# A fused memory-attention and MLP block: v's weights and the first q, k slices loaded ahead of the second 256 rows, scale steps in PSUM, finer unread products, the last tile in halves, a new order

## The chip, the cores and the metric

The kernel runs on one core of one Trainium2 chip. The metric is the device time of one execution in microseconds (us). A profile is one execution recorded by the hardware profiler. Engines: PE is TensorE (PEld its weight loads), DVE is VectorE, ACT is ScalarE, POOL is GpSimd, and SP issues DMAs. L12 is line 12 of the kernel's file; the changed file has other line numbers from L310 on (mostly one more, from L866 on five to six more).

## The reference

`x` has 2048 rows (tokens) of 512 columns. The result is the sum of three terms, all on the same rows:

```python
xn = layernorm(x)
return x + A(xn, wq, wk, wv, wo, beta) + B(xn, w1, b1, w2, b2)
# A: 32 heads of 16, 4 segments of 512 rows, run in order
for s in range(4):
    logits = qs @ ks.T / 4 + mask             # mask: -1e9 for keys behind the query
    a_dot  = softmax(logits) @ vs
    a_mem  = phi(qs) @ M / (phi(qs) @ z + 1e-6)
    o      = g * a_mem + (1 - g) * a_dot      # g = sigmoid(beta), one per head
    M, z   = M + phi(ks).T @ vs, z + phi(ks).sum(rows)
A = concat(o) @ wo                            # phi(t) = t + 1 if t > 0 else exp(t)
# B: a second layernorm, then
B = gelu(layernorm(xn) @ w1 + b1) @ w2 + b2   # 512 -> 1792 -> 512
```

## The kernel before, in words

**Number format.** Products with weights are done on f16 pairs. Each f32 matrix is split into a high part and the remainder (low part), and a product is three f16 products per block of 128 rows: high-high, high-low, low-high (`split3`, L583). So a projection of one 128-row slice of weights against 512 columns is 12 products, and so is a token tile of 128 rows against 512 columns of v's weights.

**Weights.** Before a weight can be split it has to be loaded (`w_load`, on SP's queue), its size has to be estimated from squares (`w_square`: ACT at L351, or products of blocks with themselves on PE at L380 whose diagonal DVE sums at L382; these are called traces below), and a power of two has to be made from that (`w_scale`, `qk_scale`: a small product with ones on PE, then the exponent steps at L386 and L390 on DVE). `w_split` then makes the two parts: in kind "V" ACT writes the high part (L445) and DVE the remainder (L446), in kind "G" POOL scales (L448), ACT copies (L450) and POOL subtracts (L452). The weights come in pieces: `qk` is the first 128 columns of wk and wq, `QK` the other three, `v` is wv, `1a`, `1b`, `2a`, `2b` the halves of w1 and w2, `o` is wo.

**Rows.** x comes in blocks of 256 rows (two tiles of 128). `norm_sums` and `norm_root` make mean and root, `norm_apply` normalizes, and `ln_out` transposes on PE (L561) and splits the result (L564 on ACT, L565 on DVE) into `xnT`. The first 512 rows are loaded in two blocks, the second of which is kept in the tiles nN and nD. In the kernel before the second block is normalized on POOL (L534), the first one on DVE (L532).

**Attention.** There are 16 units: 4 segments x 4 groups of 8 heads. A unit has its projections of q and k (job T, the low part Tv at L621), a round trip through DRAM that lays the heads out (`qk_rows`), the row maxima of the scores (jobs M: PE at L741, DVE at L748), their transposition (R, at L754), the scores (S at L783, exponents on ACT at L790, masks on POOL at L804), the products with v (`pv`, L817) and the normalization. For the first unit the projection of the first 256 rows stands alone (`first`, jobs Tp), ahead of that of the second 256 rows. V jobs make v for 128 tokens (12 products). The MLP runs between: jobs D (w1, evicted by DVE at L880), gelu, its split, and e (w2, L926, DVE at L930). At the end `out` multiplies by wo for a token tile (L944), DVE adds it to the tile (L947), and `save` stores it (L861).

**Order.** Nothing is scheduled automatically. Every stream of jobs (`streams`) has a letter, and the string `ORDER` says which stream is next; a job issues its instructions on the engines' queues, and each engine runs its queue in that order. A second string, `BANKS`, says which of PSUM's 8 banks each new tile (`dense`) gets; a job that gets a bank waits until the last reader of that bank is done. `hold` is a memset that makes the DMAs which reuse that memory wait for DVE. `warm` issues products of the identity with itself whose result nobody reads.

Of the kernel before, what the change touches and what calls it, by code (L numbers as in the profile page):

```python
# [9 lines left out]
F32 = mybir.dt.float32  # L10
# [22 lines left out]
NW = 8  # L33
# [25 lines left out]
def streams():  # L59
# [78 lines left out]
    "oamakrkkhbckkkk0h0bihehceddhff220ff22qhjkk2n1h1662gkkrp6237s7lg3k783w8th88999!x9u#k!w7#9$4$vRRv9R$9!3#R!#%k4J5"  # L138
    "WxkR%&RRzzz%(S%%Lz&WTzXU%Vst)L(uzz3%Tk)U&LvVYY(zTvU)z)VTz&L)Y(UYi3-YzVY*YYYk*K+-,X4zzyz**J5Y+YYYz-,6AAY-*5RAAA"
    "aBRB-RzzCBC.K.+C*C/,*A.+kAzRRR,zAA:WkRzAWz/.sRt.uzSy:TjRBwUBxBR.C.CCVCvDAbATEBFGAURwAvVARBRHxJYz/zCBCCTUICKzXA"  # L140
    "zYYzA:/VcYTURAzzsXBAz:VtiAYBvBSYYRzTzCCUuCCdDYvYz;YeEYVJT;FUVRfyRYfRY;;aATAzYbRUAzGAVYTBRcYAHzzdUBVBYeIYRSzz<z"
    "YYCCCKCz=AzYYYff>TUYYYAaAzjBsAAVtz<bYROBR<wTuyCNBCxCCA=AvDUY>RBREJPsVTYYFUGVTAuAvAHYtiwYzBzCxCBCICAzYNYRUAzAVB"
    "RYAzAvRzzzcvBCOSCBTUCCzzRYYLRDVYYEzFYzz<GzyYLYLHezATUIAMZAAAVQLBzBBWzCTCXKCCUzVAzdMJAzzsAAAMRBzMByBtCCuTCKCADA"
    "EPOwBFxAAvAvRNYZfYZfYBGUQRJBRYWCiVHKCICCzAYYzAAYBRAAzBSOYPXYYBzzzTsYzUztCuCaCCzzVYTwjxRUVTDRYYvbRzERUvVJFTURcY"
    "yWdYORYRYYSYNzeAAVYRiYTYBXYAzzYYRZUYAzAGYVRBTzzCKHBCIUCCAABVTzRWRAAXzRAUzzffRYBjVYYYTSzUQYysPBaVCCCtCADAEYBYwu"
    "AFTAGAYYxNYYBYBYQYCHCvObCICAAARvPJURABzBABszzzCCtCCLVuLTzcUVDvzzwxETdLeFzzzLGfRYYzfRHNUyVRTUVYRAAAYBRvYAAzIYMY"
    "ZBzzCBCCSKiCRAWzzaMYTYUAVzARJYbzcABABMQBYzzTUzZCCVCCTUKXsuMzYJRtDRPEyWwFxYAAAYYVGHTRQYUAABOvNIVYBRPBCCKXvCCAZA"
    "zYBYYzAAYBRAzzSjBesTzzzCCtduCUVCTDYURYYREwYzzvzxVYRTFGYJYUVYfYzRNZTyUVYYvRHRYYAAABYRYOfzAWzYSYYTYRUzAzBYYRQzzC"
    "IBCCCVzzAszAtTzURRYVAATAROWPvBUzRwRNBYyVYSXROBYCCTUXCVxCDTjAAYYYEYAFAABYGRYRYBRBHKvCIUCCCAzVATYzYYizzAsBzUzAVR"
    "QzARRTzBzBzCtCSCCPUDwLYExFYVvzGLyTYLNvLHIAAAMYzUAVzTYUYMzBzAYVMZQzZzzBCTCUOBCCAAstzzzYYYPwBWYzYAAABYVxYZNyvYBM"  # L150
    "CTCUCCvAABAYRRRDAEAzVBRFBGHRRQPWRCTCCICAjzAYUYsztAAWYXYVYzzAwvxzzBSzBXCBCTCUCDYVYTUYVYTvURYEzzVRTRYYNRRZzRRYYS"
    "FOYzUVzyATYYRUzAAGBVYYYYTHABXAzRBYUzzCCIVCCzzTAYRYUWVzAARYAzTARYBUVzBRRCSCBTUCCQDEXyVYYAAYTYFYGABPYABAYYBYHYCC"
    "UICCYAVAABYATYYBYAQUYYBCVCTUCCDEVYFYYGHYYIYYYYYYMMMZMZZZ"
# [4 lines left out]
    "01234567012345614526371052671034261705342617035426107356420735264071526540715402675430125673012657320614527036"  # L158
    "41752036475126347512034715623471625437164325741362534612054612704631720476231547361204367120436712430624751062"
    "41705241705617205436172436017236017620347620341576203145762031457632145176320475163204751632407513624057136240"  # L160
    "57162401572431507243107624531762541736257431602576403157640315640371564072561473265104765104736510427651024702"
    "63517305264137052641702614702351470623154706234710536427153642751036427513642735167340516735401564730215643725"
    "61437516437054317605431760543761054361205437205413725024513740256137425061742506314506310473152047361052170365"
    "27052431670524315627053614270361423761024671025671032567120536127410253645130243510624351067243167524316754236"
    "17542356417023564127035641270356120356142705164270514521670421657210465201476537206143720614206173540267302547"
    "03251403142650314261540356410235641027536142753641275036127503461250"
# [17 lines left out]
def infini_mixer_kernel(ctx: ExitStack, tc: tile.TileContext, x, wq, wk, wv, wo, beta, w1, b1, w2, b2, out):  # L184
# [71 lines left out]
    def col(j):  # L256
        return sc[:, j:j + 1]
# [148 lines left out]
    def w_scale(m):  # L406
# [8 lines left out]
        a = sm.tile([P, 2], F32, name="fa")  # L415
# [60 lines left out]
    def norm_root(h):  # L476
# [15 lines left out]
        nws[h] = ag, a  # L492
# [13 lines left out]
    def ratio(h):  # L506

        a = nws[h][1][:, 0]
# [351 lines left out]
    def save(tok):  # L860
        Q.dma_start(out[P * tok:P * tok + P, :], acc[tok])  # L861
# [186 lines left out]
```

## Time and profile before

| | us |
|---|---|
| median of 3 runs (lowest to highest) | 692.88 (692.62 to 693.17) |
| the profiled execution | 692.55 |
| its span, first to last instruction | 690.8 |
| PE busy | 680.1 |
| DVE busy | 504.6 |
| ACT busy | 472.2 |
| POOL busy | 353.1 |
| mean granted TensorE clock | 0.994 |

The span is 1.7 us shorter than the execution. Busy time of different engines overlaps. A matmul's duration in the profile includes its latency, so successive ones overlap as well: start to start, products of 512 columns follow at some 0.22 us, though one is recorded as 0.38. PEclk in the page is the granted clock in tenths, over 40 slices of 17 us.

### The profile page before, as it was taken

Reading aid. Unit: us, or ns where it says so; the run is one execution under the profiler, and the core shown is the slowest. Engines: PE = TensorE matmul, PEld = TensorE weight load, DVE = VectorE, ACT = ScalarE, POOL = GpSimd, SP = SyncE. Lnnn points to the kernel's source line nnn. Section 1 sums busy time; section 2 is a strip of 40 time slices with the busy share of each in tenths; the row PEclk is TensorE's granted clock in tenths of the full one; section 3 lists DMA queues with packets and bytes.
Section 4 is the critical chain, followed back from the end, with each engine's and each line's share of the span. In section 5 each row is a group of like instructions: output and inputs, shape, how many; then the busy total and the mean of one; then the engine's idle time right before and its main releaser. Section 6 shows DMA issues by size and latency. Waiting matters only on the chain.

```text
span 690.8 us, 15856 instructions
## 1 busy us (share of the span) xinstructions
PE 680.1 (98%) x5855; PEld 393.0 (57%) x5855; DVE 504.6 (73%) x1612; ACT 472.2 (68%) x877; POOL 353.1 (51%) x577
## 2 busy tenths in 40 slices
PE   6999999999999999999999999999999999999997
PEld 5854655657654566755546555565555447465543
DVE  5899978897787669867696786968577475688622
ACT  3688897987766577668836738667865555767970
POOL 7488649575535343564554345434462405438562
PEclk8999999999999999999999999999999999999999
DMA  9888233302321142322221224221402113420101
GB/s 269 264 207 205 97 94 58 99 30 76 76 47 40 34 116 58 107 48 79 69 70 26 77 57 101 70 64 44 105 18 56 55 48 94 102 77 17 18 2 61
DMA packets 52745, 55.84 MB, mean 81 GB/s; under 512 B 4974, under 2 KB 41596, under 8 KB 52668
## 3 DMA queue, kind: packets, MB, share of 16 engines
q1 hardware_dynamic: 50364, 50.64, 26.4%
q0 software_dynamic: 2304, 4.20, 3.8%
q8 instruction: 46, 0.75, 0.5%
q14 instruction: 31, 0.25, 0.1%
HBM read 37.77 MB, written 17.05 MB: 79 GB/s over the span
## 4 chain that ended last, share of the span: by engine, by line
PE 96%; POOL 1%; DVE 1%; issue 0%; POOLq 0%
PE dense L583 40%; PE dense L926 21%; PE dense L817 11%; PE dense L944 6%; PE dense L783 6%; PE dense L741 6%; PE dense L681 2%; PE dense L561 1%; PE dense L380 1%; PE dense L697 1%; PE dense L648 1%; DVE dense L748 1%; PE dense L718 1%; DVE w1s L446 0%; PE dense L754 0%; POOL kst L237 0%
## 5 line engine op out<-in xcount | busy, mean ns | idle before, releaser
L748 DVE CUSTOM_DVE_ANT_0 dense<-dense,mask 128x384 f32<-128x384 f32 (+3 forms) x512 | 233.8, 526 | 39.0 <-PE dense L741 34.4
L790 ACT ACTIVATE pt<-dense,qkcs 128x512 f32<-128x512 f32 (+1 forms) x384 | 204.0, 632 | 35.0 <-PE dense L783 35.0
L926 PE MATMUL dense<-w2s,hT 128*128 128x512 f16 x672 | 166.0, 380 | 0.0
L583 PE MATMUL dense<-xnT,w1s 128*128 128x256 f16 x1344 | 161.2, 273 | 0.0
L804 POOL TENSOR_SCALAR_AFFINE_SELECT pt<-pt 128x256 f32<-128x256 f32 x256 | 102.3, 436 | 108.8 <-ACT pt L790 108.3
L583 PEld LDWEIGHTS <-w1s 128*128 128x128 f16 x1344 | 129.5, 98 | 29.2 <-issue 5.4
L900 POOL TENSOR_TENSOR hT<-hh,hT 128x512 f16<-128x512 f32 x64 | 68.3, 1067 | 95.8 <-ACT hT L898 89.2
L926 PEld LDWEIGHTS <-hT 128*128 128x128 f16 x672 | 61.0, 98 | 67.3 <-issue 13.4
L817 PE MATMUL dense<-pt,vt 128*32 128x512 f32 (+3 forms) x1024 | 77.6, 436 | 0.0
L748 DVE DVE_READ_ACCUMULATOR2_ANT mc<- 128x1 f32 x512 | 72.6, 142 | 0.0
L880 DVE SCALAR_TENSOR_TENSOR hT<-dense,sc,cb 128x512 f32<-128x512 f32 x64 | 43.6, 681 | 34.2 <-PE dense L583 27.7
L898 ACT ACTIVATE hT<-hh 128x512 f16<-128x512 f32 x64 | 37.4, 584 | 27.1 <-POOL hh L896 27.1
L817 PEld LDWEIGHTS dense<-pt,vt 128*32 128x32 f32 x1024 | 30.7, 109 | 41.7 <-issue 31.8
L783 PE MATMUL dense<-qst,kst 50*128 50x384 f16 (+3 forms) x512 | 52.1, 298 | 1.1 <-DVE mc L748 1.1
L896 POOL TENSOR_SCALAR hh<-hT,sc 128x512 f32<-128x512 f32 x64 | 42.1, 658 | 21.2 <-ACT hT L886 17.9
L741 PE MATMUL dense<-kst,qst 48*128 48x384 f16 (+3 forms) x512 | 51.5, 298 | 0.0
L886 ACT ACTIVATE hT<-hT,b1t 128x256 f32<-128x256 f32 x112 | 46.4, 495 | 0.2
L848 POOL TENSOR_TENSOR nN<-nN,oT 128x512 f32<-128x512 f32 x16 | 21.0, 1312 | 49.5 <-DVE oT L660 49.5
L583 PE MATMUL dense<-xnT,wks 128*128 128x512 f16 (+1 forms) x252 | 44.5, 329 | 0.0
L583 PE MATMUL dense<-xnT,wqs 128*128 128x512 f16 (+1 forms) x252 | 44.4, 329 | 0.0
L944 PE MATMUL dense<-wos,oT 128*128 128x512 f16 x192 | 43.8, 379 | 0.0
L583 PE MATMUL dense<-wvs,xnT 128*128 128x512 f16 x192 | 43.8, 379 | 0.0
(230 smaller groups left out, 838.1 us busy)
## 6 DMA issues: line engine op xcount, KB each, us to landing
kst<-kd SPq DMA_DIRECT2D x32, 192.0 KB
qst<-qd SPq DMA_DIRECT2D x32, 192.0 KB
qd<-hl SPq DMA_DIRECT2D x36, 128.0 KB
kd<-hl SPq DMA_DIRECT2D x33, 128.0 KB
acc<-in_A_x_dram SPq DMA_DIRECT2D x16, 256.0 KB
acc<-in_B_b_dram POOLq DMA_DIRECT2D x16, 256.0 KB, 4.2
out_dram<-acc SPq DMA_DIRECT2D x16, 256.0 KB
xt<-in_A_x_dram SPq DMA_DIRECT2D x14, 256.0 KB
```

Source lines behind the costliest of these rows:

```text
L583: T.matmul(p, ws(k, a), xs(k, b), start=i == 0, stop=i == 3 * KT - 1)
L741: T.matmul(p[:, o:o + n], stk[i, 0][r, t, P * qb:P * qb + P], stk[i, 1][r, t, :n], start=True, stop=True)
L748: V.tensor_tensor_reduce(p[:, o:o + n], p[:, o:o + n], mask[:, 512 - n:], 1.0, -3e38, OP.add, OP.max, mc[i][:, 4 * b + t, qb:qb + 1])
L783: T.matmul(p[:, o:o + n], stk[i, 1][r, t, P * kb:P * kb + P], stk[i, 0][r, t, P * kb:], start=True, stop=True)
L790: A.activation(pt[i, 4 * b + t][:, OFF[kb]:OFF[kb] + n], p[:, c:c + n], AF.Exp, scale=qkcs[:, 1, i % NG:i % NG + 1])
L804: G.affine_select(v, v, pattern=[[0, 2], [1, P]], compare_op=OP.is_ge, fill=0.0, base=0, channel_multiplier=-1)
L817: T.matmul(p[32 * c:32 * c + 32, P * kb:], vt[s, kb][:, 4 * g + c, 16 * odd:16 * odd + 32], pt[i, 2 * c + odd][:, OFF[kb]:OFF[kb] + LEN[kb ...
L880: V.scalar_tensor_tensor(hzs[fh][:, f0:f + 1, :], p[:, :256 * n].rearrange("p (f c) -> p f c", f=n), col(CG + fh), cbt[hf].unsqueeze(1).to ...
L886: A.activation(hzs[j % 2][:, f, :], hzs[j % 2][:, f, :], AF.Gelu_apprx_tanh, bias=b1t[:, fo:fo + 1])
L900: G.tensor_tensor(hT[:, z, 1, :], hht[j, c], hT[:, z, 0, :], op=OP.subtract)
L926: T.matmul(p, t[:, u, P * a:P * a + P], w2s[:, fo, v, :], start=fi == 0 and n == 0, stop=fi == FH - 1 and n == 2)
L944: T.matmul(p, o[:, u, P * b:P * b + P], wos[:, g, v, :], start=i == 0, stop=i == 3 * NG - 1)
```

## The change

**Loads.** The loads were one stream; now each weight has its own (`load` + name), so that their order can be chosen freely. Before, SP's queue begins with all 512 rows, then the four slices of wk and wq, then wv:

```order
L546 DMA xt<-in_A_x_dram 128x512 x2
L546 DMA nN<-in_A_x_dram 128x512
L546 DMA nD<-in_A_x_dram 128x512
L290 DMA wks<-in_A_wk_dram 128x4x128
L290 DMA wqs<-in_A_wq_dram 128x4x128
L290 DMA wks<-in_A_wk_dram 128x4x128
L290 DMA wqs<-in_A_wq_dram 128x4x128
L290 DMA pt<-in_A_wk_dram 128x4x128
L290 DMA pt<-in_A_wq_dram 128x4x128
L290 DMA pt<-in_A_wk_dram 128x4x128
L290 DMA pt<-in_A_wq_dram 128x4x128
L318 DMA wvs<-in_A_wv_dram 128x2x512
```

The same place in the changed kernel (wvs and pt hold pieces of v's weights here, in wks, wqs and pt those of k and q; nN and nD are the second 256 rows):

```order
L547 DMA xt<-in_A_x_dram 128x512 x2
L318 DMA wvs<-in_A_wv_dram 128x2x512
L290 DMA wks<-in_A_wk_dram 128x4x128
L290 DMA wqs<-in_A_wq_dram 128x4x128
L310 DMA pt<-in_A_wv_dram 128x512 x2
L290 DMA wks<-in_A_wk_dram 128x4x128
L290 DMA wqs<-in_A_wq_dram 128x4x128
L290 DMA pt<-in_A_wk_dram 128x4x128
L290 DMA pt<-in_A_wq_dram 128x4x128
L547 DMA nN<-in_A_x_dram 128x512
L547 DMA nD<-in_A_x_dram 128x512
L290 DMA pt<-in_A_wk_dram 128x4x128
```

Half of v (512 KB) took the place of the second 256 rows, the rest of v follows the first slices, and the second rows come after three of the four slices of k and q.

**DVE in the start.** Before, from the memset of `hold` to the first weight splits; L472 and L473 are the means, L565 the splits of transposed rows, L382 the diagonal of wv's or wk's trace:

```order
L532 TENSOR_SCALAR xt<-xt,ag,stats 128x512 x2
L565 SCALAR_TENSOR_TENSOR xnT<-dense_224,xnT 128x4x128
L565 SCALAR_TENSOR_TENSOR xnT<-dense_231,xnT 128x4x128
L386 TENSOR_SCALAR fa<-dense_248 128x2
L390 TENSOR_SCALAR qksc<-fa 128x2 x4
L403 TENSOR_TENSOR qkcs<-qksc 128x1
L404 SCALAR_TENSOR_TENSOR qkcs<-qksc 128x1
L565 SCALAR_TENSOR_TENSOR xnT<-dense_258,xnT 128x4x128
L565 SCALAR_TENSOR_TENSOR xnT<-dense_265,xnT 128x4x128
L382 SCALAR_TENSOR_TENSOR dense_238,am<-dense_238,ident 128x128
```

Now:

```order
L533 TENSOR_SCALAR xt<-xt,ag,stats 128x512 x2
L386 TENSOR_SCALAR dense_250<-dense_250 128x2
L390 TENSOR_SCALAR qksc<-dense_250 128x2 x4
L403 TENSOR_TENSOR qkcs<-qksc 128x1
L404 SCALAR_TENSOR_TENSOR qkcs<-qksc 128x1
L566 SCALAR_TENSOR_TENSOR xnT<-dense_263,xnT 128x4x128
L382 SCALAR_TENSOR_TENSOR dense_224,am<-dense_224,ident 128x128
L566 SCALAR_TENSOR_TENSOR xnT<-dense_279,xnT 128x4x128
L386 TENSOR_SCALAR dense_291<-dense_291 128x1
L390 TENSOR_SCALAR sc<-dense_291 128x1 x2
L446 SCALAR_TENSOR_TENSOR wks<-wks,qksc 128x512
L446 SCALAR_TENSOR_TENSOR wvs<-wvs,sc 128x512 x2
```

The scale steps read and write the PSUM tile (`dense`) in place of the small SBUF tile `fa`, they stand ahead of the first rows' splits, and the splits of wv follow at once; the second rows' splits stand later, behind two V jobs on PE.

**PE in the start and behind it.** Two of the four V jobs of the first segment, and the first 16 of the 28 blocks of w2's first trace, stand ahead of the second unit's q projection (the first one over 512 columns) instead of behind it. In both kernels the MLP's first jobs and the first two units' row maxima follow.

**DVE ahead of the second unit's row maxima**, where the last splits of w1 and wq, the sum of a w2 job (L930), the first unit's transposed maxima (L757) and a copy of the memory (L721) stand. Before:

```order
L446 SCALAR_TENSOR_TENSOR wqs<-pt,qksc,wqs 128x512
L757 SCALAR_TENSOR_TENSOR mhl<-dense_941,mhl 32x128
L930 SCALAR_TENSOR_TENSOR acc<-dense_855,sc,acc 128x512
L446 SCALAR_TENSOR_TENSOR w1s<-w1s,sc 128x512
L721 COPY mst<-dense_969 128x32
L748 ISA dense_993,mc<-dense_993,mask 128x512
```

Now:

```order
L446 SCALAR_TENSOR_TENSOR wqs<-pt,qksc,wqs 128x512
L446 SCALAR_TENSOR_TENSOR w1s<-w1s,sc 128x512
L935 SCALAR_TENSOR_TENSOR acc<-dense_885,sc,acc 128x512
L758 SCALAR_TENSOR_TENSOR mhl<-dense_1019,mhl 32x128
L722 COPY mst<-dense_1025 128x32
L749 ISA dense_1044,mc<-dense_1044,mask 128x512
```

The same five steps stand there; the split of w1 moved ahead of the w2 sum and of the first unit's maxima.

**The rest.** `warm` issues 24 times 2 products in place of 8 times 4. For both blocks of the first 512 rows the root alone is taken at first, the second factor moves to `ratio`, and the second block is normalized on DVE like the first. The last token tile's product with wo is done in two halves of 256 columns, each with its own addition on DVE and its own store.

The diff, cut to its core (of the two strings only the first line):

```diff
-NW = 8
+NW = 24
...
     for m in PARTS:
-        put("loads", *[("wl", m, k) for k in range(LOADS[m])])
+        put("load" + m.lower(), *[("wl", m, k) for k in range(LOADS[m])])
         if m == "qk":
-            put("loads", ("hold",))
+            put("loadqk", ("hold",))
         if m == "v":
-            put("loads", ("par",))
+            put("loadv", ("par",))
...
 ORDER = (
-    "oamakrkkhbckkkk0h0bihehceddhff220ff22qhjkk2n1h1662gkkrp6237s7lg3k783w8th88999!x9u#k!w7#9$4$vRRv9R$9!3#R!#%k4J5"
+    "xhhahuhhblk6hhlwk6hkchkhhadhhhkh$hemmhhh6if$f8$7hhjhh%s8%7%8lg%8xbtR88ceRd8gff&&9r99n!#!&y&C(nzv(D+()(C*(o)BB+"
...
 BANKS = (
-    "01234567012345614526371052671034261705342617035426107356420735264071526540715402675430125673012657320614527036"
+    "01234567012345670123456012345723651476025176025413706254143750624375062147506214756031475603175604157360415273"
...
     def qk_scale(g0, n):
-        h = sm.tile([P, 2], F32, name="fa")
+        h = p[:, 4:6]
...
     def w_scale(m):
-        a = sm.tile([P, 2], F32, name="fa")
+        a = p[:, 6:8]
...
     def norm_root(h):
         G.tensor_scalar(a[:, 0], ag[:, :, 1], EPS, 0.0, op0=OP.add, op1=OP.add)
-        if h == 0:
+        nws[h] = ag, a
+        if h < 2:
             G.tensor_tensor(r[:, 0], a[:, 0], mhalf[:, :2], op=OP.pow)
+            return
         G.tensor_scalar(a[:, 1], ag[:, :, 1], 1.0 + EPS, EPS * EPS, op0=OP.mult, op1=OP.add)
-        if h == 0:
-            G.tensor_tensor(r[:, 3], a[:, 1], mhalf[:, :2], op=OP.pow)
-            nws[h] = ag, a
-            return
...
     def warm(n):
-        for k in range(4):
-            T.matmul(p[:, :256], b[:, :P], b, start=k == 0, stop=k == 3)
+        for k in range(2):
+            T.matmul(p[:, :256], b[:, :P], b, start=k == 0, stop=k == 1)
...
     def ratio(h):
+        if h < 2:
+            G.tensor_scalar(b[:, 1], ag[:, :, 1], 1.0 + EPS, EPS * EPS, op0=OP.mult, op1=OP.add)
+            G.tensor_tensor(stats[:, h % 4, 3], b[:, 1], mhalf[:, :2], op=OP.pow)
...
     def norm_apply(h, j, t):
-        if h == 0:
+        if h < 2:
             V.tensor_scalar(t, t, nws[h][0][:, j, 0:1], r[:, 0, j:j + 1], op0=OP.subtract, op1=OP.mult)
...
+    def halves(tok):
+        return (slice(0, 256), slice(256, 512)) if tok == 4 * NSEG - 1 else (slice(0, 512),)
+
     def save(tok):
-        Q.dma_start(out[P * tok:P * tok + P, :], acc[tok])
+        for c in halves(tok):
+            Q.dma_start(out[P * tok:P * tok + P, c], acc[tok][:, c])
...
                 p = dense()
                 t = acc[tok]
-                V.scalar_tensor_tensor(t, p, col(CO), t, op0=OP.mult, op1=OP.add)
+                for c in halves(tok):
+                    i = 0
+                    for g in range(NG):
+                        o = oT[NG * s + g]
+                        for u, v in ((0, 0), (0, 1), (1, 0)):
+                            T.matmul(p[:, c], o[:, u, P * b:P * b + P], wos[:, g, v, c], start=i == 0, stop=i == 3 * NG - 1)
+                            i += 1
+                    V.scalar_tensor_tensor(t[:, c], p[:, c], col(CO), t[:, c], op0=OP.mult, op1=OP.add)
```

More of the change, by code (lines that the diff above doesn't have):

```diff
@@ L154 @@
+    "X4BKXXXL4F4XEX214YXZFF0G41ZM04441ZFGG440344GHGFNX1HZH40FOF1FIIIIFZG44XG0FHGX4FGGH4HXFXXIYE1ZIII0J1WK4Z4GG4LVMH"
+    "4G44GHGHN4W40O4II3I1ZIGG444GH44G4G404HHI1ZII0IJK14LM4444444N4O44S5SS5S55"
 )
 BANKS = (
[L158 to L160 removed]
@@ L939, in go @@
                 p = dense()
-                i = 0
-                for g in range(NG):
-                    o = oT[NG * s + g]
-                    for u, v in ((0, 0), (0, 1), (1, 0)):
-                        T.matmul(p, o[:, u, P * b:P * b + P], wos[:, g, v, :], start=i == 0, stop=i == 3 * NG - 1)
-                        i += 1
-                t = acc[tok]
-                V.scalar_tensor_tensor(t, p, col(CO), t, op0=OP.mult, op1=OP.add)
+                t = acc[tok]
+                for c in halves(tok):
[6 more added lines that the diff above has]
+                    V.scalar_tensor_tensor(t[:, c], p[:, c], col(CO), t[:, c], op0=OP.mult, op1=OP.add)
             return go
```

46 lines of the change are left out of this document (23 added, 23 removed).

## The prediction

> **What bounds the kernel now.** I read the page first, then windows by stage, then the chain of waits at the start and the end, then the timeline of single instructions. The page and the grouped chain:
>
> ```profile
> span 690.8 us, 15856 instructions
> ...
> PE 680.1 (98%) x5855; PEld 393.0 (57%) x5855; DVE 504.6 (73%) x1612; ACT 472.2 (68%) x877; POOL 353.1 (51%) x577
> ...
> PEclk8999999999999999999999999999999999999999
> ...
> PE 96%; POOL 1%; DVE 1%; issue 0%; POOLq 0%
> ```
>
> PE is busy for 98% of the span, so time can only come from PE's work, from its first 27 us, or from its few waits. The windows say where PE is not alone:
>
> ```profile
> core 0: us, PE busy (x) PEld busy (x) DVE busy (x) ACT busy (x) POOL busy (x), PEclk, DMA share, GB/s
> 6.40:9.80 3.40, 1.17 (x12) 1.14 (x12) 2.11 (x6) 1.92 (x5) 2.94 (x9) 1.00 1.16 304
> 9.80:16.70 6.90, 5.65 (x37) 5.04 (x35) 4.76 (x11) 2.23 (x6) 4.98 (x10) 0.51 1.15 322
> 16.70:26.90 10.20, 10.17 (x113) 8.90 (x112) 8.35 (x36) 5.69 (x11) 1.82 (x2) 1.00 1.09 316
> 26.00:89.10 63.10, 62.03 (x541) 37.02 (x540) 59.41 (x202) 52.76 (x100) 45.19 (x53) 1.00 0.63 168
> 100.00:200.00 100.00, 100.00 (x943) 60.63 (x941) 83.11 (x269) 80.99 (x154) 61.97 (x108) 1.00 0.30 72
> ```
>
> Up to 16.7 us PE has gaps, and from 9.8 us its granted clock is 0.51. From 16.7 us on it is full. From 26 to 89 us, where weights are still being split and the first two units' row maxima run, DVE is busy 59.41 of 63.10 us (94%): nearly a second bound. Later it has 17% to spare. The sum is therefore made at three places: when PE reaches the first 512-column projection, when it reaches the second unit's transposition of maxima (R1 below), and the end.
>
> **The start.** Rows of the timeline (start in us, duration, engine, line, operation, what it wrote and read; in brackets the idle time ahead and who ended it), and below them the chain of waits (start, duration, PE line, number of products):
>
> ```profile
> 8.45 0.63 ACT L351 ACTIVATE wqs<-wqs 128x512 bf16<-128x512 f32 x1 [0.15 <-DMA wqs<-in_A_wq_dram]
> ...
> 17.87 0.46 PEld L380 LDWEIGHTS <-pt 128*128 128x128 bf16 x8 [0.19 <-DMA pt<-in_A_wv_dram]
> ...
> 11.44 1.70 DVE L390 TENSOR_SCALAR qksc<-fa 128x2 int32<-128x2 int32 x4
> ...
> 20.55 0.39 DVE L390 TENSOR_SCALAR qksc<-fa 128x6 int32<-128x6 int32 x4
> ...
> 12.02 1.07 POOL L227 MEMSET vt<- 128x256 f32 x4
> ...
> 17.17 0.71 ACT L445 ACTIVATE wqs<-wqs,qksc 128x512 f16<-128x512 f32 x1
> ...
> 17.52 0.75 DVE L446 SCALAR_TENSOR_TENSOR wks<-wks,qksc 128x512 f16<-128x512 f32 x1
> 18.18 0.75 DVE L446 SCALAR_TENSOR_TENSOR wqs<-wqs,qksc 128x512 f16<-128x512 f32 x1
> ...
> 26.91 2.32 PE L583 MATMUL dense<-xnT,wqs 128*128 128x512 f16 x10
> ```
>
> ```profile
> 18.51 1.31 PE dense L583 x12
> ...
> 25.18 0.80 PE dense L380 x14
> ...
> 27.04 2.61 PE dense L583 x12
> 29.66 1.60 PE dense L380 x28
> ```
>
> Loads first. The queue moves 256 KB in about 0.81 us at the 322 GB/s of the window. The first q slice lands at 8.45. In the new order the same number of bytes stands ahead of it (512 KB of v in place of 512 KB of x), so it still lands then. Behind it come v's other two slices, two k/q pairs and the second 256 rows: eight transfers, 6.5 to 7 us, so the second rows land at 15 to 15.6 instead of under 7, and v's last slice at about 10.1 instead of 17.87. Moving the second rows back costs nothing itself, because their transpositions now stand behind two v jobs on PE (below); if v came late, it would not matter either.
>
> Scale steps in PSUM: the four L390 at 11.44 read only the SBUF tile and took 1.70 us while POOL's norm and memsets ran; the same four at 20.55 took 0.39 with POOL quiet. In PSUM I take 0.4. That removes 1.3 us from DVE ahead of the first weight split. [...]
>
> Norm of the second rows on DVE: two operations, 0.97 us in all by the first rows' pair, at about 20.2, where DVE is waiting for PE's two v jobs; POOL loses as much. The `pow` that moves to `ratio` stays on POOL. Of no cost.
>
> Unread products: 48 instead of 32, of 0.11 us each at full clock, but 32 of them stand before anything else can run; of the rest all but two fill PE's gaps before 16.7 us. The one W job that stands behind the start costs 0.22 us.
>
> Now PE's path by the order. Scale steps end at 10.3, `wf` of v at 11.75; ACT's first split 12.4; then six DVE splits (wks, two of v, wqs, two of v) with a pitch of 0.66 us (17.52 to 18.18) that end at 17.4. The first v job is paced by them and ends at 17.9. From there PE has no gap to speak of: v job 2 (2.61), q's projection (1.31), four traces of 4 products (0.46 in all), 8 transpositions (0.9), the two w1 traces (2 x 0.80), the two second-row projections (2 x 1.31), small ones (0.8) and 16 of the 28 products of w2's trace (0.92): 11.2 us, so the 512-column projection starts at about 29.15 instead of 26.91: +2.25.
>
> What is taken from behind it: two v jobs (5.2), the 16 products (0.92), less 0.22, so 5.9 us. PE alone would be at R1 after 63.17 (26.91 to 90.08) - 5.9 - 1.4 (a wait, below) = 55.9 us, at 85.05 instead of 90.08.
>
> **DVE in the first 90 us.** DVE can't follow PE that far:
>
> ```profile
> 26.02 0.30 DVE L382 SCALAR_TENSOR_TENSOR dense<-dense,ident 128x128 f32<-128x128 f32 x1 [0.52 <-PE dense L380]
> ...
> 88.92 0.14 DVE L748 DVE_READ_ACCUMULATOR2_ANT mc<- 128x1 f32 x1
> ...
> 90.08 0.27 PE L754 MATMUL dense<-ident,mc 128*32 128x128 f32 x1
> ```
>
> Two groups of the same stretch (number of instructions, busy time and mean in ns, idle time ahead of them):
>
> ```profile
> L748 DVE CUSTOM_DVE_ANT_0 dense<-dense,mask 128x512 f32<-128x512 f32 (+3 forms) x64 | 29.2, 525 | 0.3 <-PE dense L741 0.2
> ...
> L880 DVE SCALAR_TENSOR_TENSOR hT<-dense,sc,cb 128x512 f32<-128x512 f32 (+1 forms) x8 | 5.4, 678 | 1.6 <-PE dense L583 1.4
> ```
>
> From w1's trace (26.02) to the last row maximum of the second unit (89.06) DVE needed 63.04 us in before. In the new order the same stretch starts at 25.3 and has nearly the same work: one more split (wqs) and one fewer (wvs), and besides them the small gate steps, the copy of b1 and little else, 0.9 us by the same steps of before. The 64 row maxima alone are 29.2 us, without the reading of their results. If it goes as before, the last maximum is done at 25.3 + 63.04 + 0.9 = 89.2. Some of DVE's idle time was waiting for PE (1.6 us ahead of L880), and PE is earlier now; I take off half, 0.8: 88.4. R1 then starts behind the PE job in progress (half of a 1.31 us job): 89.1, against 90.08, **-1.0**. The bounds: 86.3 with no idle time at all (25.3 + 59.4 + 0.9 + 0.65), 92.6 with two more blocked splits (rival 2).
>
> What I weigh most is this block by POOL:
>
> ```profile
> 68.01 2.50 DVE L446 SCALAR_TENSOR_TENSOR w1s<-w1s,sc 128x512 f16<-128x512 f32 x1
> ...
> 66.72 1.45 POOL L452 TENSOR_TENSOR w1s<-w1s 128x512 f16<-128x512 f32 x1
> ...
> 68.52 1.43 POOL L452 TENSOR_TENSOR wks<-pt,wks 128x512 f16<-128x512 f32 x1
> ...
> 71.86 0.64 PE L783 MATMUL dense<-qst,kst 50*128 50x384 f16 x7 [1.05 <-DVE mc L748]
> ```
>
> A split that took 0.75 at 17.52 took 2.50 here, while POOL ran three steps of its own splits back to back (an L448 stands between the two rows); PE then waited 1.05 us for a row maximum. So each such meeting costs DVE 1.75 us. [...]
>
> Behind R1 the jobs are the same in another order, PE was full and DVE had 17% to spare: 0, between -0.5 and +1.
>
> **The end.** The last token tile in two halves; the rows of the chain and the timeline there:
>
> ```profile
> 679.94 6.71 PE dense L944 x31
> ...
> 686.67 0.75 DVE L947 SCALAR_TENSOR_TENSOR acc<-dense,sc,acc 128x512 f32<-128x512 f32 x1 [1.84 <-PE dense L944]
> ...
> 684.86 2.92 SPq L861 DMA_DIRECT2D out_dram<-acc  x2
> ```
>
> and, by shape, the last line's products (min, median and max in ns, first and last start) and the only DVE step of such a kind over 256 columns:
>
> ```profile
> L944 PE MATMUL dense<-wos,oT x192: 379/379/390, 213.2 to 686.2; 128*128 128x512 f16 x192
> ...
> L880 DVE SCALAR_TENSOR_TENSOR hT<-dense,sc,cb 128x256 f32<-128x256 f32 x16 | 7.7, 483 | 9.0 <-PE dense L583 8.8
> ```
>
> 24 products of 256 columns cost what 12 of 512 did (1.31 for 12, 2.61 for 12). But the halves share one PSUM tile, and in the new order the second half's first product waits for DVE's add of the first half: 0.31 us until DVE can begin (from the last product's start, 686.2, to DVE's, 686.67, it is 0.42 to 0.47; 0.11 less for half the columns), its 0.48 (a 256-column step, 483 ns), less the 0.11 of a product's own turn: +0.68. It can't be a gain, since PE has nothing else to do there; with DVE's full 0.75 it would be 0.95. Behind the last product, the add is 0.48 instead of 0.75 and starts 0.11 earlier: -0.38. The store is 128 KB instead of 256: between 0 and -0.4 (half of 0.81), I take -0.3. The end together: **0.0**.
>
> **The sum.** -1.0 + 0 + 0.0 = -1.0 on the profiled execution, whose span of 690.8 and 1.7 around it make 692.55; the median of the runs, 692.88, is 0.33 above. So 691.9. A measurement of this kernel can tell about 0.2% (1.39 us) from no change, so 691.5 to 694.3 counts as the same.
>
> **The rivals.** (1) DVE keeps up: the splits now stand apart from POOL's and DVE is hardly idle (0.5 us left): R1 at about 86.8, -3.3, 689.6. For it: 3.7 us of idle time in the window and one block alone worth 1.75. Against it: 94% over 63 us with 29 us of row maxima in pairs that wait for PE, and PE for their banks.
> (2) Slower: the early splits put POOL's and DVE's w1 and w2 splits nearer together. DVE has no slack, so a block goes to PE in full. It decides from the second additional one: 2 x 1.75 brings R1 to 92.6, +2.5, so 695.4. For it: the row at 68.01; on DVE's new queue two splits stand directly ahead of the second unit's maxima. Against it: before had the same number of splits and one block of this size.
> (3) The clock isn't held: in 6.4 to 9.8 PE was busy 1.17 of 3.40, and in the next 6.9 us it got 0.51. With the new products about 2 of 3.4 are busy. If that isn't enough, the first k projection (1.31) and part of the first v job run at half clock, +1.3 to +2.4 at the start and so at DVE's: 693.2 to 694.3. [...]
> That the halves gain nothing is in the forecast.
>
> **How the numbers follow.** Forecast 0.38 (its own range 690.8 to 693.4), rival 1 0.33, rival 2 0.17, rival 3 0.12, half of it above the bound. Faster 0.33, same 0.38 + 0.06 = 0.44, slower 0.17 + 0.06 = 0.23. The range reaches from rival 1 to rival 2, 689.3 to 695.4.
>
> **What would show it.** In the profile of the changed kernel: PEclk near 1.0 between 9.8 and 16.7; four L390 in 0.4 us; the first 512-column projection at about 29.15; R1 at 89.1 with PE waiting for DVE in the second unit's maxima or their banks; DVE busy for 95% or more from 25 to 88; one wait of about 0.7 us for DVE ahead of the last 12 products. I am wrong if R1 is before 87.5 or after 91, if waits for DVE appear behind 100 us, or if the start is not within 0.7 us of 29.15.

## The result, and the profile after

The changed kernel takes 694.51 us (median of 15 runs, 693.11 to 695.73), the kernel before 692.28 (15 runs, 691.70 to 693.17): a ratio of 1.0031, with a 95% interval of 1.0023 to 1.0039. It is slower by 0.3%, where 691.9 was forecast. The profiled execution took 693.23 (span 691.5), one of the shortest. So there are two questions: why even this one is 0.68 longer than the profiled one before (692.55), and why most of the others are longer still.

Parts 1 and 2 of its page, as shown of the kernel before:

```profile
span 691.5 us, 15930 instructions
...
PE 681.1 (98%) x5883; PEld 393.9 (57%) x5883; DVE 503.2 (73%) x1615; ACT 471.5 (68%) x877; POOL 348.4 (50%) x574
...
PEclk9999999999999999999999999999999999999999
```

The windows of the prediction, with the one from 25 us on (columns as there):

```profile
6.40:9.80 3.40, 2.15 (x23) 1.53 (x21) 1.00 (x2) 1.45 (x4) 3.02 (x8) 1.00 1.11 349
9.80:16.70 6.90, 6.35 (x64) 5.34 (x65) 5.62 (x19) 5.18 (x9) 1.41 (x2) 1.00 1.18 310
16.70:26.90 10.20, 10.20 (x93) 7.56 (x91) 8.63 (x29) 4.19 (x10) 3.46 (x5) 1.00 1.07 299
25.00:88.80 63.80, 61.75 (x556) 38.96 (x554) 60.48 (x210) 52.59 (x102) 45.21 (x56) 1.00 0.62 163
100.00:200.00 100.00, 99.96 (x941) 60.36 (x940) 82.92 (x275) 80.31 (x153) 61.54 (x106) 1.00 0.31 80
```

The start has the full clock now, and DVE is again busy for 95% of the stretch up to R1. The single steps that the prediction named, from the timeline:

```profile
10.30 0.36 DVE L390 TENSOR_SCALAR qksc<-dense 128x2 int32<-128x2 int32 x4
...
29.38 0.38 PE L584 MATMUL dense<-xnT,wqs 128*128 128x512 f16 x1
...
88.74 0.27 PE L755 MATMUL dense<-ident,mc 128*32 128x128 f32 x1
```

The scale steps take 0.36 us instead of 1.70, although POOL runs a memset over all of that time (9.32 to 11.27); whether PSUM or the kind of POOL's instruction makes the difference was not tested. The first 512-column projection starts at 29.38, R1 at 88.74. Where the two profiled executions part, worked out from the starts of the same jobs on PE (us):

| stage on PE | before | after | |
|---|---|---|---|
| to the first 512-column projection | 26.91 | 29.38 | +2.47 |
| from there to R1 | 63.17 | 59.36 | -3.81 |
| from R1 to the last segment's first product with wo (P below) | 585.81 | 587.27 | +1.46 |
| from there to the span's end | 14.91 | 15.49 | +0.58 |
| span | 690.8 | 691.5 | +0.7 |

R1 is 1.34 earlier, and that is given back: 1.46 behind it and 0.58 at the end. PE's waits, of the changed kernel (engine, line waited at, who ended it, us, times, longest):

```profile
PE dense L742 <- DVE acc L935: 1.7, 1, 1.7
...
PE dense L951 <- DVE acc L953: 0.6, 1, 0.6
...
PE dense L784 <- DMA qst<-md: 0.4, 1, 0.4
```

The second row is the wait between the halves; the third is a wait for a transfer behind R1, which run 7 comes back to. The first stands at 63 us, among the second unit's row maxima (L742), which need the PSUM bank that DVE's sum of a w2 job (L935) still reads. DVE, POOL and PE there:

```profile
61.88 0.95 DVE L446 SCALAR_TENSOR_TENSOR wqs<-pt,qksc,wqs 128x512 f16<-128x512 f32 x1
62.75 1.64 DVE L446 SCALAR_TENSOR_TENSOR w1s<-w1s,sc 128x512 f16<-128x512 f32 x1
64.32 0.74 DVE L935 SCALAR_TENSOR_TENSOR acc<-dense,sc,acc 128x512 f32<-128x512 f32 x1
...
62.24 1.61 POOL L452 TENSOR_TENSOR wks<-pt,wks 128x512 f16<-128x512 f32 x1
...
65.11 0.56 PE L742 MATMUL dense<-kst,qst 48*128 48x512 f16 x2 [1.75 <-DVE acc L935]
```

Two weight splits stand ahead of the sum on DVE's queue, and they take 0.95 and 1.64 us instead of 0.74 each, with POOL working between them. PE waits 1.75 us; the longest wait of the kernel before behind its first 15 us was 1.05.

The last tile:

```profile
685.61 0.48 DVE L953 SCALAR_TENSOR_TENSOR acc<-dense,sc,acc 128x256 f32<-128x256 f32 x1 [0.56 <-PE dense L951]
686.14 1.47 PE L951 MATMUL dense<-wos,oT 128*128 128x256 f16 x12 [0.57 <-DVE acc L953]
...
687.65 0.48 DVE L953 SCALAR_TENSOR_TENSOR acc<-dense,sc,acc 128x256 f32<-128x256 f32 x1 [1.56 <-PE dense L951]
```

From the last addition's start to the span's end it is 3.85 us, against 4.13 before: 0.28 won, all of it the shorter addition. (Run 3's profile, with the tile in one piece, has 4.55 there, so whether the smaller store gains something too stays open.) Up to that start the wait has cost more.

One thing the times themselves show: of the 15 executions, four had a mean granted clock of 1.000 and took 693.11 to 693.82; the eleven others, at 0.996 to 0.998, took 693.84 to 695.73.

### The profile page after: what moved, and what is told of

It is laid out like the page before. It is cut to its first block, busy times and chain, and to the rows that moved or that the text cites. A ratio compares the mean times of both kernels' runs of the same rounds, so it can differ in the third digit from the quotient of the medians.

```text
span 691.5 us, 15930 instructions
## 1 busy us (share of the span) xinstructions
PE 681.1 (98%) x5883; PEld 393.9 (57%) x5883; DVE 503.2 (73%) x1615; ACT 471.5 (68%) x877; POOL 348.4 (50%) x574
## 4 chain that ended last, share of the span: by engine, by line
PE 91%; DVE 3%; DMA 2%; POOL 1%; ACT 1%; issue 1%; SPq 0%; POOLq 0%; DVEq 0%
PE dense L584 38%; PE dense L931 19%; PE dense L818 10%; PE dense L784 6%; PE dense L951 6%; PE dense L742 5%; PE dense L682 2%; DMA oT<-in_B_w_dram 1%; PE dense L562 1%; DVE dense L749 1%; PE dense L698 1%; PE dense L649 1%; PE dense L380 1%; DMA md<-mhl 0%; PE dense L719 0%
## 5 line engine op out<-in xcount | busy, mean ns | idle before, releaser
L805 POOL TENSOR_SCALAR_AFFINE_SELECT pt<-pt 128x256 f32<-128x256 f32 x256 | 100.0, 420 | 122.1 <-ACT pt L791 121.7
L742 PE MATMUL dense<-kst,qst 48*128 48x384 f16 (+3 forms) x512 | 52.1, 298 | 1.9 <-DVE acc L935 1.7
L784 PE MATMUL dense<-qst,kst 50*128 50x512 f16 (+3 forms) x512 | 52.1, 298 | 0.4 <-DMA qst<-md 0.4
L951 PE MATMUL dense<-wos,oT 128*128 128x512 f16 (+1 forms) x204 | 44.0, 367 | 0.8 <-DVE acc L953 0.6
```

Source lines behind the costliest of these rows:

```text
L742: T.matmul(p[:, o:o + n], stk[i, 0][r, t, P * qb:P * qb + P], stk[i, 1][r, t, :n], start=True, stop=True)
L784: T.matmul(p[:, o:o + n], stk[i, 1][r, t, P * kb:P * kb + P], stk[i, 0][r, t, P * kb:], start=True, stop=True)
L805: G.affine_select(v, v, pattern=[[0, 2], [1, P]], compare_op=OP.is_ge, fill=0.0, base=0, channel_multiplier=-1)
L951: T.matmul(p[:, c], o[:, u, P * b:P * b + P], wos[:, g, v, c], start=i == 0, stop=i == 3 * NG - 1)
```

## The experiments

All runs are compared with runs of the kernel before on the same chip (its medians there: 692.42 to 692.72). "Full clock" is an execution with a mean clock of 0.999 or 1.000; 0.999 counts because in ten of the fourteen profiles the clock falls in the last 0.3 to 2.1 us of the span, behind PE's last product, which takes up to 0.0015 off the mean (in the kernel before's it is 0.50 from 689.5 to the span's end, 690.8).

**1. The control.** The changed kernel, unedited.

> The changed kernel once more, as the control of this batch. Theory C (clock): its executions divide by the granted clock; those with a mean clock of 1.000 take about 693.2 us (the profiled one did), those with 0.996 to 0.998 take 694.4 to 695.7, because in them PE's start runs at half clock for one window or so; the median is near 694.5. Rival O (other cause: transfers or POOL blocking DVE in the first 90 us in some executions): the same spread, but without a link to the clock; a profile of a longer execution shows full clock in the first 20 us and longer DVE steps.

694.26 us (693.74 to 695.63; ratio 1.0032, 1.0020 to 1.0044). Two of five executions at full clock, 693.74 and 693.81. This time the profile fell on a long one (695.25), and its windows say where the clock went. It isn't the start:

```profile
64.00:66.00 2.00, 0.16 (x3) 0.04 (x1) 2.00 (x3) 2.00 (x7) 2.00 (x2) 1.00 0.00 1
66.00:67.00 1.00, 1.00 (x7) 0.50 (x7) 1.00 (x5) 0.61 (x2) 0.26 (x1) 0.91 0.02 5
67.00:70.00 3.00, 3.00 (x16) 2.07 (x15) 3.00 (x13) 0.00 (x0) 0.48 (x1) 0.50 0.61 152
70.00:71.00 1.00, 1.00 (x9) 0.76 (x8) 0.93 (x6) 0.00 (x0) 0.42 (x1) 0.88 0.96 336
```

The clock (the number behind POOL's) is halved from 66.8 to 70.2: 2 x (0.09 + 3 x 0.50 + 0.12) = 3.4 us. It follows the wait for the w2 sum, in which PE did nothing from 64.1 to 65.95:

```profile
62.09 1.59 DVE L446 SCALAR_TENSOR_TENSOR wqs<-pt,qksc,wqs 128x512 f16<-128x512 f32 x1
63.60 1.64 DVE L446 SCALAR_TENSOR_TENSOR w1s<-w1s,sc 128x512 f16<-128x512 f32 x1
...
61.97 1.16 POOL L452 TENSOR_TENSOR w1s<-w1s 128x512 f16<-128x512 f32 x1 [1.33 <-ACT w1s L450]
63.09 1.61 POOL L452 TENSOR_TENSOR wks<-pt,wks 128x512 f16<-128x512 f32 x1
64.65 1.60 POOL L452 TENSOR_TENSOR w1s<-w1s 128x512 f16<-128x512 f32 x1
...
65.95 0.56 PE L742 MATMUL dense<-kst,qst 48*128 48x512 f16 x2 [1.84 <-DVE acc L935]
66.45 4.46 PE L584 MATMUL dense<-xnT,w1s 128*128 128x256 f16 x24
```

The 24 products behind it take 4.46 us. The same 24 in the first profile of the changed kernel, at full clock:

```profile
65.60 2.79 PE L584 MATMUL dense<-xnT,w1s 128*128 128x256 f16 x24
```

So PE loses 1.7 us there. R1 is at 90.89 in this profile, 61.08 behind the first 512-column projection instead of 59.36; a part of that goes with DVE's first split, 1.59 instead of 0.95 (run 2 tells the two apart). So the expectation named the right sign (the clock) and the wrong place.

**2. The start's gap filled.** This had been set up for that wrong place.

```diff
     def warm(n):
-        for k in range(2):
-            T.matmul(p[:, :256], b[:, :P], b, start=k == 0, stop=k == 1)
+        m = 12 if n == 18 else 2
+        for k in range(m):
+            T.matmul(p[:, :256], b[:, :P], b, start=k == 0, stop=k == m - 1)
```

> The changed kernel with 10 more unread products in the job W18, which stands ahead of PE's 1.06 us gap at 8.64; they take 10 x 0.109 = 1.1 us and PE would have been idle there. Theory C: PE is busy about 3.2 of 3.4 us between 6.4 and 9.8, every execution keeps the full clock, the spread shrinks below 1 us, and the median falls by about 1.2 to 693.2 to 693.5. Rival O: no change of median or spread (694.5 within 0.4).

693.88 (692.07 to 695.95; ratio 1.0022, 1.0011 to 1.0032), and still 8 of 12 executions below full clock. PE is busy for all of 6.4 to 9.8 in its profile, and the spread stays: the start isn't the cause. The profile shows something else. The two splits take 1.59 and 1.64 us as in run 1, PE waits for the w2 sum even longer, and yet the clock stays full behind it (L743 and L936 are L742 and L935 here; the columns of the second row as above):

```profile
65.93 0.56 PE L743 MATMUL dense<-kst,qst 48*128 48x512 f16 x2 [2.17 <-DVE acc L936]
...
66.00:72.00 6.00, 6.00 (x47) 3.98 (x46) 5.86 (x26) 2.41 (x7) 1.12 (x2) 1.00 0.64 174
```

From the first 512-column projection to R1 it is 59.87 here, 59.36 in the first profile, 61.08 in run 1. So the longer split goes with 0.5 us, and the halved clock with 1.2 of the 1.7 that PE loses.

**3 and 4. The last tile in one piece, and in two PSUM tiles.**

```diff
     def halves(tok):
-        return (slice(0, 256), slice(256, 512)) if tok == 4 * NSEG - 1 else (slice(0, 512),)
+        return (slice(0, 512),)
```

```diff
                 for c in halves(tok):
+                    if c.start:
+                        p = dense()
                     i = 0
```

> The changed kernel with the last token tile in one piece of 512 columns again. By the profile of the changed kernel, the last tile's first product is 0.23 later than before and the span's end 0.7 later, so the halves cost 0.47: the median falls by 0.5 against the control (694.0). If the smaller store and the shorter addition make up for the wait (my prediction: 0.0), it stays at 694.5.

> The changed kernel with the second half of the last tile in a PSUM tile of its own (another bank), so that its products don't wait for the first half's addition. The wait was 0.57 us in the profile: the median falls by 0.6 against the control (693.9), and is below that of the whole tile by 0.1 to 0.2. If the time of the halves lies in the two stores instead, it stays within 0.2 of the control.

In one piece 694.21 (1.0024, 1.0015 to 1.0034), in two tiles 692.99 (1.0013, 1.0004 to 1.0022), the control 694.26. The clock's lottery is in these medians; the executions at full clock alone have means of 693.5 (six of the changed kernel, in both batches), 693.3 (three, one piece) and 692.8 (six, two tiles). So the wait between the halves costs 0.7, and the halves as they were written gain nothing against one piece (0.2 is within the spread). With two tiles the second half's products follow at once, and the last addition starts 1.31 us behind that of the first half instead of 2.04:

```profile
685.10 0.48 DVE L955 SCALAR_TENSOR_TENSOR acc<-dense,sc,acc 128x256 f32<-128x256 f32 x1 [0.56 <-PE dense L953]
686.41 0.48 DVE L955 SCALAR_TENSOR_TENSOR acc<-dense,sc,acc 128x256 f32<-128x256 f32 x1 [0.83 <-PE dense L953]
```

**5. PE kept busy in the wait at 63 us.** The new theory (W): the half clock comes from that wait. In run 1, 3.4 us at half clock follow a wait of 1.84 us, in run 3 as many follow one of 2.21; behind 1.75 us in the first profile and 2.17 in run 2 there are none, and what picks the executions was not shown. If W holds, no execution without the wait is at half clock there, and the median is near 693.4. ("The gate" in run 9's expectation is whatever grants PE its clock.) The edit puts 16 unread products into the second unit's memory job, right ahead of the maxima that wait.

```diff
     def kv(i):
+        if i == 1:
+            f = ident.bitcast(BF)
+            for k in range(16):
+                T.matmul(p[:, 256:], f[:, :P], f, start=k == 0, stop=k == 15)
         if s == 0:
             V.tensor_copy(mst[:, g, :], p[:, :32])
```

> The changed kernel with 16 unread products (1.74 us) on PE in the second unit's memory job, right ahead of the row maxima where PE otherwise waits 1.7 us for DVE's w2 sum; DVE's and POOL's work is the same. [...] Rival D (the longer executions come from DVE or POOL and the clock is only a sign of it): the spread and the median of 694.3 stay.

693.16 (692.54 to 694.17; ratio 1.0005, 0.9997 to 1.0014). All eleven executions are at full clock.

```profile
63.30 1.92 PE L724 MATMUL dense<-ident 128*128 128x256 bf16 x16
65.15 1.07 PE L746 MATMUL dense<-kst,qst 48*128 48x512 f16 x8
```

The maxima start when they did (65.15 and 65.11), the DVE splits take as long (0.96 and 1.64), R1 is at 89.17. Products that nobody reads, in time that PE would have waited, are worth 1.1 us of the median. That confirms W. D isn't the whole cause, since the edit leaves DVE's and POOL's work as it was; a part of it stays, the 0.5 of run 2.

**6. The cause of the wait moved.** Jobs around the second unit's first maxima (M), by their order in the string; `split` is a job on ACT and DVE, `scale` one on POOL:

```diff
 maxima of unit 0, last two jobs
-split of the last slice of wq
 w2 jobs 4 and 5
-split of w1's piece 8, scale of piece 9
 w2 jobs 6 to 10, R of unit 0, memory job of unit 1
 M 0 of unit 1
+split of w1's piece 8, scale of piece 9
 M 1 of unit 1
 M 2 of unit 1
+split of the last slice of wq
```

> The changed kernel with two of DVE's weight splits (the last of wq, the second of w1's second half) moved from ahead of the w2 sum to behind the second unit's first maxima, and POOL's scaling of the next w1 piece with them. Theory W: PE's wait for the w2 sum shrinks from 1.7 us to under 0.5, the clock stays full, median 693.3. As DVE has the same work, the second unit's transposition of maxima stays at 88.7 within 0.5 in the profile; if DVE isn't what sets it, it comes 1.2 earlier.

691.96 (691.46 to 692.80; ratio 0.9990, 0.9982 to 0.9999). All eleven at full clock. Its DVE and PE rows:

```profile
61.83 0.75 DVE L935 SCALAR_TENSOR_TENSOR acc<-dense,sc,acc 128x512 f32<-128x512 f32 x1
...
64.39 0.74 DVE L446 SCALAR_TENSOR_TENSOR w1s<-w1s,sc 128x512 f16<-128x512 f32 x1
...
67.84 0.75 DVE L446 SCALAR_TENSOR_TENSOR wqs<-pt,qksc,wqs 128x512 f16<-128x512 f32 x1
...
62.71 1.31 PE L742 MATMUL dense<-kst,qst 48*128 48x512 f16 x8
```

PE doesn't wait at these maxima any more, and the two splits have their usual 0.74 us: they hardly meet POOL's subtractions (only for 0.2 us, from 64.94 on, at the end of the first). That is 1.1 us less on DVE, and R1 is at 87.49, 1.25 earlier than in the changed kernel's profile. So the alternative in the expectation (R1 1.2 earlier) came, but not because DVE doesn't set it: DVE lost the time to POOL.

**7. The kernel before's order behind R1.** Jobs, order and banks behind R1 are those of the kernel before; seven small jobs differ in which side of R1 they are on.

> The changed kernel up to the second unit's transposition of maxima, and behind it all jobs in the order (and the PSUM banks) of the kernel before. Between the two profiles the changed order lost 1.46 us there (598.2 against 596.55 from that transposition to the last tile). If that is the order's doing, the span shrinks by about 1.4 and the median falls to 692.9 with the clock's loss still in it, 691.8 in executions at full clock. If the loss belongs to the state that the start leaves behind (later weights, other transfers), it stays and so does 694.3.

693.88 (692.59 to 695.67; ratio 1.0016, 1.0007 to 1.0026), 9 of 12 executions below full clock; the three at full clock have a mean of 692.9. From R1 to P it is 586.84 instead of 587.27. That alone says little, since the ten profiles with the changed order (the first one and runs 1 to 6, 9, 10 and 12) have 586.46 to 587.70 there. Of the 1.03 that remain against 585.81, 0.81 lie between R1 and the third unit's transposition, at the seam where the two orders were joined (one wait there is for a copy of ACT):

```profile
PE dense L525 <- ACT mhl L757: 0.4, 1, 0.4
```

Behind that transposition it is 549.4, against 549.2 before and 550.5 to 551.7 in those ten profiles, which have 0.7 more work there (one D job instead of one w2 job). So the later order does cost something, 0.6 to 1.8, and this join gave most of it back at the seam. What differs among the ten is one wait for a transfer, in the first profile (above) and not in run 2 (below):

```profile
371.01 1.17 PE L784 MATMUL dense<-qst,kst 50*128 50x512 f16 x8 [0.41 <-DMA qst<-md]
...
371.32 0.82 PE L785 MATMUL dense<-qst,kst 50*128 50x512 f16 x8
```

Five of the ten wait there (the first one and runs 1, 3, 4 and 6), and the stretch between two transpositions of maxima in which it lies takes 40.1 to 40.7 us; in the five others it takes 39.5, and R1 to P is 586.5 to 586.6. So 0.8 of the first profile's +1.46 come from this wait, which not every execution has. What makes the other 0.7 isn't settled.

**8. All three together:** the edits of 6, 7 and 4.

> The changed kernel with the moved DVE splits, the kernel before's order behind the second unit's transposition of maxima, and the last half in a PSUM tile of its own. If the three effects add up: no half clock (-1.0), order (-1.4), tile (-0.6 to -0.75) off 694.3: 691.2, which is below the kernel before (692.5) by 1.3, 0.2%. If the moved splits only shift the wait, 692.2.

690.18 (690.03 to 691.09, five runs; ratio 0.9962, 0.9950 to 0.9974). This version is faster than both kernels. R1 is at 87.32, from R1 to P 586.31, from there to the end 14.67, a span of 688.3. It is 1.0 below the 691.2 expected: for the edit of 6 the expectation counted the clock alone, and the earlier R1 comes on top.

**9. A shorter gap:** 8 unread products in place of the 16 of run 5.

```diff
-            for k in range(16):
-                T.matmul(p[:, 256:], f[:, :P], f, start=k == 0, stop=k == 15)
+            for k in range(8):
+                T.matmul(p[:, 256:], f[:, :P], f, start=k == 0, stop=k == 7)
```

> The changed kernel with 8 unread products (0.87 us) in place of 16 at the same place, so that PE waits about 0.9 us instead of 1.75. Theory W: a gap of 0.9 us is too short for the gate (the kernel before has one of 1.05 us at 70.8 and shows no half clock there), so no execution is below 0.999 and the median is 693.2 as with 16. [...]

693.61 (692.56 to 695.52; ratio 1.0018, 1.0008 to 1.0028): seven executions at full clock (mean 693.1) and five at 0.996 or 0.997 (mean 695.1). The profile is one of the long ones:

```profile
66.90 0.56 PE L746 MATMUL dense<-kst,qst 48*128 48x512 f16 x2 [1.41 <-DVE acc L939]
...
68.00:72.00 4.00, 4.00 (x23) 2.87 (x21) 3.90 (x19) 0.00 (x0) 0.89 (x1) 0.57 0.69 196
```

Here the wait was 1.41, not 0.9, since DVE's splits took 1.59 and 1.64, and that was enough: the clock of 68 to 72 us is 0.57. The expectation of a harmless 0.9 was not tested, because the wait varies with how DVE and POOL meet. The same profile also waits 1.4 us for a transfer at 42 to 44 us (0.5 in run 3, under 0.2 in the others with this order), so its length isn't the clock's alone.

**10 and 12. POOL's subtraction moved.** In run 10 a job on POOL, the subtraction of a piece of wk, was moved behind the third of the second unit's maxima jobs. No other POOL work stands between the two places, so POOL's queue stayed as it was; the run is a second control.

> The changed kernel with one POOL subtraction (a piece of wk, 1.16 us, at 62.24) moved behind the second unit's first maxima; DVE's order is unchanged. Theory P (DVE's two splits took 0.95 and 1.64 there instead of 0.74, because POOL ran between them, and DVE sets when the second unit's maxima end): the two splits take at most 1.8 us together, PE's wait for the w2 sum falls from 1.75 to about 0.9, the second unit's transposition comes 0.8 to 1.1 earlier (87.6 to 87.9 in the profile), the clock stays full, the median is 692.3 to 692.6. If the block isn't POOL's doing, the splits stay at 2.4 together and the median at 694.3. If POOL's step only blocks DVE a little later, the transposition stays at 88.7 and the median falls to 693.2 by the clock alone.

693.97 (692.50 to 696.06; ratio 1.0023, 1.0013 to 1.0033), 7 of 11 executions below full clock; the splits took 1.59 and 1.64. In run 12 the job went one step further, behind the subtraction of w1's piece 9:

```diff
 POOL: subtraction of w1's piece 7
-POOL: subtraction of a piece of wk
 POOL: subtraction of w1's piece 9
+POOL: subtraction of a piece of wk
```

> The changed kernel with POOL's subtraction of a wk piece (62.24 in its profile) moved behind POOL's next one, of a w1 piece; in the run before (e10) the move stopped ahead of that and left POOL's queue as it was. DVE's order is unchanged. Theory P (POOL's back-to-back subtractions block DVE's two splits, and DVE sets when the second unit's maxima end): POOL is idle for most of 62.3 to 64.4, the two splits take at most 1.8 us together (2.6 to 3.2 in the profiles of the changed order so far), PE's wait for the w2 sum is 0.6 to 0.9 us instead of 1.75, the transposition of the second unit's maxima comes 0.8 to 1.2 earlier (87.5 to 87.9), no execution is at half clock there, and the median is 692.3 to 692.7. If the block isn't POOL's doing, splits, wait and median (694.3) stay. If POOL only blocks the next DVE steps, the transposition stays at 88.7 and only the clock's part is won: 693.2.

692.36 (691.20 to 694.25; ratio 0.9999, 0.9990 to 1.0008); one of eleven executions is below full clock (0.997).

```profile
62.02 1.16 POOL L452 TENSOR_TENSOR w1s<-w1s 128x512 f16<-128x512 f32 x1 [1.34 <-ACT w1s L450]
64.63 1.16 POOL L452 TENSOR_TENSOR w1s<-w1s 128x512 f16<-128x512 f32 x1 [1.46 <-ACT w1s L450]
...
62.13 1.59 DVE L446 SCALAR_TENSOR_TENSOR wqs<-pt,qksc,wqs 128x512 f16<-128x512 f32 x1
63.64 0.74 DVE L446 SCALAR_TENSOR_TENSOR w1s<-w1s,sc 128x512 f16<-128x512 f32 x1
...
65.10 0.56 PE L742 MATMUL dense<-kst,qst 48*128 48x512 f16 x2 [1.23 <-DVE acc L935]
```

The second split, whose POOL neighbour is gone, took 0.74 in place of 1.64. The first one still met a subtraction (1.59), so together they took 2.33, and the wait is 1.23: shorter than 1.75, not 0.6 to 0.9. R1 is at 88.42, not at 87.5 to 87.9. It stands 58.72 behind the first 512-column projection, instead of 59.36 in the first profile and 59.87 in run 2, whose first split took 1.59 too. So DVE's gain arrives there, and the median came out as expected although splits, wait and R1 were forecast better than they are. That POOL's subtractions block these splits is shown.

**11. The halves alone**, in two PSUM tiles, put into the kernel before (the code of the change and the edit of run 4).

> The kernel before with the last tile in halves, the second in a PSUM tile of its own: this part of the change alone, without its wait. From the addition of the tile before the last to the span's end it took 6.72 us in the profile before and 6.51 in that of the changed kernel with two tiles, so the median falls by 0.2, to 692.4 if the kernel before has 692.6; not clear of the noise. If the two smaller stores gain what half a store's bytes are worth, it falls by 0.4.

692.28 against 692.56 (ratio 0.9993, 0.9984 to 1.0001): 0.3 us, not clear of the noise, as expected.

## Why the prediction was wrong

Of 691.9 forecast and 694.51 measured, 2.6 are missing (with the kernel before at 692.28 in the later runs, 3.2). Point by point:

- **The start**: right. 29.38 instead of 29.15, L390 in 0.36, the full clock from 9.8 to 16.7. That it is the PSUM tile that takes 1.3 us off L390 is shown by no run; the profile shows the 0.36 beside POOL's memsets (9.32 to 11.27). Rival 3 as it was put, a half clock in the start, is in no profile with the changed start.
- **DVE in the first 90 us**: right in size for the profiled execution. R1 at 88.74, forecast 89.1; DVE set it, as run 6 shows, where 1.1 us less on DVE moved R1 by 1.25. PE's own time, 85.05, was not what set it; the prediction took 1.4 off it for a wait whose row shows 1.05, which is without consequence. The block by POOL, rival 2's mechanism, was there, at the place that rival named (the two splits ahead of the second unit's maxima): 1.1 us in one profile, 1.75 in others. It was within the forecast's margin for R1.
- **The step that failed: what PE's wait costs.** The prediction counted a wait of PE as its length only, in the term "-1.0" for R1, and looked for a halved clock only in the start (rival 3). Behind the wait of 1.4 to 2.2 us at 63 to 67 us the clock was halved in five of eight profiles (0.50 from 67 to 70 us in run 1, 3.4 us in all). PE then loses 1.7 us, of which 0.9 to 1.2 reach R1 (from the first projection 61.08 and 60.77 in runs 1 and 10, against 59.87 in run 2 with the same splits). Of the changed kernel's 20 executions in its own series and the control, 14 were below full clock, with a mean of 694.9 against 693.5 for the six others: +1.4 in such an execution (with what else differs in them, as the longer split), and 1.0 of the median. Run 5 takes the clock's part away and nothing else (693.16), run 6 the wait (691.96).
- **Behind R1**: forecast 0, between -0.5 and +1; measured +1.46 in the first profile, +0.65 to +1.9 in the ten. Mis-sized. That it was "the same jobs" didn't make them cost the same: behind the seam, run 7 with the old order takes 549.4 and the changed one 550.5 to 551.7, of which 0.7 is more work. One wait for a transfer is 0.8 of the +1.46; the cause of the rest stays open.
- **The end**: forecast 0.0, measured +0.47 for the last tile. The addition in halves gained 0.28 in all; the store's -0.3 was not there between these two profiles, and the last addition started 0.75 later behind the tile's first product (3.55 us instead of 2.80), forecast +0.57. With two PSUM tiles it is a gain of about 0.2 in the profiles of runs 4 and 11, not clear of the noise in run 11's times.

So the sum of the profiled execution is -1.34 + 1.46 + 0.58 = +0.7, and what varies between executions, the clock above all, makes the other part of the +2.2 of the median. The measured median lies inside the prediction's range, but that is no merit of its mechanism: the wide upper end came from a rival that wanted two more blocked splits at R1, and R1 came early. (The range's lower end, 689.3, should have been rival 1's 689.6.)

## What to carry to other kernels

A wait of the busiest engine isn't worth its length: here one wait of 1.4 to 2.2 us on TensorE was followed by half clock in five of eight profiles, for 3.4 us in runs 1, 3, 9 and 10. So look for the longest gap, and read several executions' clocks before believing one profile. If the gap can't be removed, unread products in it cost nothing here (run 5: the maxima behind them start at 65.15 instead of 65.11), but half as many were not enough (run 9). When work is moved ahead of a sum that frees a PSUM bank, count what queues behind it on that engine, and whether GpSimd works beside it: here splits of 0.74 us took 0.95 to 1.64 beside its subtractions.

## What the runs showed of the hardware that was not expected

- **How short a gap is enough.** Profiled executions with a gap of 1.41 (run 9), 1.84 (run 1), 1.90 (run 10), 2.0 (run 7) and 2.21 us (run 3) got half the clock behind it; gaps of 1.05 (the kernel before), 1.23 (run 12), 1.74 (run 4), 1.75 (the changed kernel) and 2.17 (run 2) in other executions didn't. So the length alone doesn't decide. What else does was not shown. In runs 1, 3, 9 and 10 the share of the clock that is missing there adds up to 1.7 us, that is 3.4 us at half clock (66.8 to 70.2 in run 1).
- **DVE and POOL hold each other up.** In run 1, two DVE splits that take 0.74 us alone and two POOL subtractions that take 1.16 are recorded with about 1.6 each. DVE's steps end 0.55 us behind the end of a POOL step (63.13 to 63.68, 64.70 to 65.24), POOL's 1.0 behind the end of a DVE step (63.68 to 64.70, 65.24 to 66.25). So in these rows the two seem to take turns. The 2.50 us at 68.01 in the kernel before stay the exception: that split, too, ends 0.56 behind the end of a POOL subtraction (69.95 to 70.51), but POOL began two instructions after the one that it ran into.
- **A half clock that costs nothing.** Of 57 executions of the kernel before in two batches, the 30 with a mean clock of 0.994 to 0.996 took 692.6 us on average and the 11 at 0.999 or 1.000 took 692.8; the 11 at 0.997 or 0.998 took 692.2. (The five at 0.991 or 0.992 took 693.3; no profile shows where their clock was low.) Its profile has the half clock in the start, at 9.8 to 16.7 us. Run 11 has the same start, and its profile has the full clock there; the first 512-column projection starts at 27.10 and 26.91 all the same, R1 at 90.26 and 90.08. So in that start something other than PE's clock sets the time.
